# A delta-rule attention block and a hard-swish MLP on one core: eleven quarter products with w_in from the third block on, the sums of w_in moved to VectorE, and preparations moved between steps

## The chip, the cores and the metric

The kernel runs on one core of one Trainium2 chip. The metric is the device time of a launch in microseconds (us), as the median of several launches of the same program. TensorE (PE in the profile; PEld are its weight loads) multiplies matrices into PSUM. VectorE (DVE), ScalarE (ACT) and GpSimd (POOL) work beside it, and SyncE (SP) issues most of the DMAs. Each engine takes its instructions in the order in which the program lists them. An instruction that needs another engine's result waits for a semaphore, and all that is queued behind it on its own engine waits too.

## The reference

The first half is a delta rule over 768 tokens, for 4 batches and 8 heads of width 48. The second half is an MLP over the 3072 tokens that come out.

```python
k_n = k / (norm(k) + 1e-06)
for t in range(S):
    y[:, :, t] = einsum('bhd,bhde->bhe', q[:, :, t], state)
    v_old = einsum('bhde,bhd->bhe', state, kt)
    state = state + bt[:, :, :, None] * einsum('bhd,bhe->bhde', kt, vt - v_old)
x = y.transpose(0, 2, 1, 3).reshape(B * S, H * D)        # 3072 x 384
h = x @ w_in                                             # 384 x 2048
g = h * clip(h + 3.0, 0.0, 6.0) / 6.0
out = g @ w_out                                          # 2048 x 384
```

## The kernel before

**Chunks and steps.** The sequence is cut into 24 chunks of 32 tokens; a chunk of all four batches has 128 token rows. The loop at the end of the kernel has one *step* per chunk, from step 5 on; what comes before step 5 follows a written list of words (`ORDER`). In step t these parts are interleaved by hand in 15 *units* (u = 0 to 14):

- the chain of chunk t (`chain`): `ks` is the product with the state in unit 0; `R` is made on VectorE in units 1 and 2 and `y` in unit 3; `pz` follows in unit 4; the state's update `su` and the output product `py` in unit 8; `y` and the state's new value are made on VectorE in unit 9; `yt` transposes y in unit 10, and ScalarE copies it to `xT`, which is the MLP's input.
- the preparation of a later chunk (`prep`), in five stages: `kb` (the scaled keys, on GpSimd); four transposes of the keys (`pt`), their copy `KQ` on ScalarE and the `mask` (two GpSimd products into `mb`, which has one buffer); four transposes of the queries; the scores (`sc`, 64 small products); and `L` and `LB`, two VectorE products that read the scores and the mask, with `bkb` on GpSimd behind them. The stages are taken one by one: `now` is taken in units 1, 2, 4, 5 and 6, and the first stage of the next preparation (`later`) in unit 13. In a step that is listed in `APART`, scores and products come in units 6 and 7 in place of 4 and 5.
- a unit of the MLP (`mlp_units`) in each of the 15 units.
- *fill*: the norms of the keys of a later group of four chunks (four pairs of a GpSimd square `sq` and a VectorE sum `ss`, where `sq` has one buffer), or the inversion of the triangular matrices of the next group (`inverse`: a VectorE transpose of 1024 columns, 60 small VectorE products and subtractions, and a transpose back). Its pieces are spread over the units by a planned cost (`room`, `due`).

The scores of all preparations, `ks` and `su` share two PSUM slots (ring `pc`): `ks` and `su` each take both of them. All other products share four (ring `pm`). A slot is free when the instruction that reads it is done.

**The MLP.** A block is two chunks (256 tokens), so a block takes two steps. Its first half is `up`: for each of 16 column tiles of w_in there are 3 matmuls of 256 columns, and each of them is two instructions in the trace (96 for a block). ScalarE and VectorE then make the activation. `up_by_eleven` makes the same by a Strassen-like scheme: for each of 8 pairs of column tiles (j) there are seven products of 128 columns and two of 256 (18 instructions; 144 for a block). It takes 16 units, as `up` does. `begin(j)` issues four of the products, ScalarE copies them out, and GpSimd makes two sums (L1030, in `plus_minus`); `end(j)` issues the other five, then VectorE adds twice (L1093, L1097), and ScalarE and VectorE make the activation (L1110, L1113). It needs sums of w_in (`weight_sums`: S1, S2, S4, and W21 in place) and of the block's tokens (`token_sums`, on VectorE in unit 11). `UF` is the first block that is made this way.

The second half of a block is `down`; from block 2 on it is `down_by_seven`, a Strassen scheme with 7 of 8 products, in 14 units. It needs sums of w_out: 12 VectorE pieces (`quarters`, L1197) and four more in place (`last_quarter`, L1203). Block 1 still uses the plain `down` of 16 units; four of these come before step 5. In step 5 the units 0 to 11 are the rest of block 1's `down`, and block 2's `up` starts in unit 12. Each later block starts its `up` in unit 12 of an odd step as well.

**Places that the prediction names.** Before the change, steps 5 and 6 take two preparations each (chunks 9 and 10, then 11 and 12) and all later steps one. The inversion for chunks 9 to 12 (group 3) starts in unit 0 of step 7; in later groups it starts in unit 6 of the second step of a group (`ready`).

Of the kernel before, what the change touches and what calls it, by code (L numbers as in the profile page):

```python
# [44 lines left out]
def kernel(  # L45
# [969 lines left out]
                past.add(("up", blk))  # L1015
            yield

    UF = 4
    S1, S2, S4 = (sums_in[:, i] for i in range(3))

    def w_tiles(s, i):
# [7 lines left out]
    def plus_minus(out, a, b, op):  # L1029
        nc.gpsimd.tensor_tensor(out=out, in0=a, in1=b, op=op)  # L1030

    def weight_sums():
        for j in range(0, NPR, 2):
            r = slice(j, j + 2)
            plus_minus(S1[:, r], W21[:, r], W22[:, r], ALU.add)
            yield
            plus_minus(S2[:, r], S1[:, r], W11[:, r], ALU.subtract)
            yield
            plus_minus(S4[:, r], W12[:, r], S2[:, r], ALU.subtract)
            yield  # L1040
            plus_minus(W21[:, r], W11[:, r], W21[:, r], ALU.subtract)
            yield

    def x_tiles(blk):
        x = xTs[blk]
# [13 lines left out]
    def up_by_eleven(blk):  # L1059
        needs(("sums", blk))  # L1060
        B11, T3x, B21, B22, _, _ = x_tiles(blk)
        B3 = xTs[blk][:, 2].rearrange("p (i c) -> p i c", c=P)
        phs, ready = {}, {}

        def mm(ph, n, w, x, start=False, stop=False):
            nc.tensor.matmul(  # L1066
                ph[:, n], lhsT=w, rhs=x, start=start, stop=stop, skip_group_check=True
            )

        def begin(j):  # L1070
            key = ("ph", blk, "by", j)
            ring("pm", NPM, key)
            ph = phs[j] = psM.tile([128, 4, P], FP32, name="ph", tag=slot["pm"])
            mm(ph, 0, W11[:, j], B11, start=True)
            mm(ph, 1, S1[:, j], T1x)
            mm(ph, 2, W21[:, j], T3x)
            mm(ph, 3, S2[:, j], T2x)
            gs[blk, j] = g_all[:, 2 * j : 2 * j + 2]
            gt = gs[blk, j].rearrange("p i (t c) -> p (i t) c", c=P)
            nc.scalar.activation(out=gt, in_=ph[:], func=ACTF.Copy)  # L1080
            plus_minus(gt[:, 3:1:-1], gt[:, 0:2], gt[:, 3:1:-1], ALU.add)
            plus_minus(gt[:, 0], gt[:, 0], gt[:, 2], ALU.add)

        def end(j):
            ph = phs.pop(j)
            mm(ph, 0, W12[:, j], B21)
            mm(ph, 1, S4[:, j], B22)
            mm(ph, 2, W22[:, j], T4x)
            mm(ph, slice(0, 2), W13[:, j], B3)
            mm(ph, slice(2, 4), W23[:, j], B3, stop=True)  # L1090
            g = gs[blk, j].rearrange("p i c -> p (i c)")
            gt = gs[blk, j].rearrange("p i (t c) -> p (i t) c", c=P)
            nc.vector.tensor_tensor(  # L1093
                out=gt[:, 1:3], in0=ph[:, 1:3],
                in1=gt[:, 3].unsqueeze(1).to_broadcast([128, 2, P]), op=ALU.add,
            )
            nc.vector.tensor_tensor(out=gt[:, 3], in0=ph[:, 3], in1=gt[:, 0], op=ALU.add)  # L1097

            def first():
                nc.scalar.activation(out=gt[:, 0], in_=ph[:, 0], func=ACTF.Copy)  # L1100
                read(("ph", blk, "by", j))
                if j == 0 and blk < 9:
                    ready[j] = second
                else:
                    second()

            def second():
                ro = mlp.tile([128, CB, DM], FP32, name="o", bufs=1)
                r = ro[:].rearrange("p c m -> p (c m)")[:, 0 : 2 * TB]
                nc.scalar.activation(out=r, in_=g, func=ACTF.Relu, bias=half, scale=1.0 / 6.0)  # L1110

                def rest():
                    nc.vector.scalar_tensor_tensor(  # L1113
                        out=g, in0=r, scalar=1.0, in1=g, op0=ALU.min, op1=ALU.mult
                    )

# [12 lines left out]
        begin(1)  # L1129
        yield  # L1130
        for j in range(NPR):
            end(j)
            go(j - 1)
            if j + 2 < NPR:
                yield
                begin(j + 2)
                if j == 1:
                    go(0)
                go(j)
                yield  # L1140
# [156 lines left out]
    def mlp_units():  # L1297
# [21 lines left out]
        for blk in range(1, N // CB):  # L1319
            mode["of"] = "down"  # L1320
            mode["mean"] = 0.72 if blk + 1 < UF else 0.4
            sums = weight_sums() if blk == UF - 1 else iter(())
            for _ in downs(blk):
                next(sums, None)
                next(sums, None)
                yield
            if blk + 1 < N // CB:
                mode["of"] = "eleven" if blk + 1 >= UF else "up"
                for n, _ in enumerate((up_by_eleven if blk + 1 >= UF else up)(blk + 1)):
                    if blk + 1 == FIRST and n >= HF:  # L1330
                        drain(rest)
                        if n % 2:
                            last_quarter(n - HF - 1)
                    yield


# [9 lines left out]
    def drain(gen):  # L1346
        for _ in gen:
            pass
# [9 lines left out]
    def prep_of(t):  # L1358
        return made(("p", t), lambda: prep(t), t < N)
# [92 lines left out]
    with tc.manual_schedule():  # L1452
# [11 lines left out]
        loads = iter(())  # L1464
        left = due = 0
        USED = {"up": 0.42, "eleven": 1.0, "down": 0.7}
        APART = (12,)
        CHAIN = {0: 0.45, 1: 0.75, 2: 0.75, 3: 0.4, 4: 0.4, 6: 0.5, 9: 0.8, 10: 0.6, 14: 0.2}
        for t in range(LS, N):
            g, i = group(t)  # L1470
            ch = chain_of(t)
            behind = t - LS < LA - LE
            first_of = t + min(LA, LE + t - LS)
            now, more, later = (prep_of(first_of + n) for n in range(3))
            if not behind:
                more, later = (), more
            take(gens["v"], 4)
            if i == 0:
                left += 1
# [15 lines left out]
                13: lambda: take(later),  # L1495
            }
            if behind:
                for u in (7, 8, 10, 11, 12, 13):
                    plan[u] = lambda ch=plan.get(u): (ch and u < 13 and ch(), take(more))
                plan[14] = lambda: take(later)  # L1500
            ready = (2, 0) if behind or i == 2 and t - LS == LA - LE else (1, 6)
            for u in range(NU):
                if u in plan:
                    plan[u]()
                take(loads, 2)
                if (i, u) == (0, 2):
# [21 lines left out]
                due = min(due, 2.6)  # L1528
                take(fill, int(due))
                left, due = max(left - int(due), 0), due - int(due)  # L1530
            drain(ch)
        for _ in units:
            settle(2)
# [30 lines left out]
```

## Time and profile before

| what | us |
|---|---|
| median of 3 launches | 664.71 |
| lowest and highest of the 3 | 663.36, 664.77 |
| the profiled launch, its own time | 662.4 |
| the profiled launch, span from first to last instruction | 660.6 |
| TensorE busy | 633.3 |
| VectorE busy | 492.7 |
| ScalarE busy | 276.7 |
| GpSimd busy | 217.0 |

The profiled launch took 662.4 us, of which 660.6 us lie between its first and last instruction. In the lines below a time is in us from the start of that span. In the windows, the numbers of each stretch are the busy time of each engine, with the number of its instructions in brackets. In the timeline a line is: start, length, engine, line of the kernel, operation, tiles written and read, shape, count, and in square brackets the idle time of the engine just before and what ended it. The mean clock that TensorE was granted is 0.982.

The steps start, by the first `ks` matmul, at 152.6 (step 5), 179.9 (6), 207.2 (7), 232.8 (8), 258.6 (9), 283.8 (10), 308.6 (11), 333.7 (12) and 358.7 (13).

### The profile page before, as it was taken

Reading aid. Unit: us, or ns where it says so; the run is one execution under the profiler, and the core shown is the slowest. Engines: PE = TensorE matmul, PEld = TensorE weight load, DVE = VectorE, ACT = ScalarE, POOL = GpSimd, SP = SyncE. Lnnn points to the kernel's source line nnn. Section 1 sums busy time; section 2 is a strip of 40 time slices with the busy share of each in tenths; the row PEclk is TensorE's granted clock in tenths of the full one; section 3 lists DMA queues with packets and bytes.
Section 4 is the critical chain, followed back from the end, with each engine's and each line's share of the span. In section 5 each row is a group of like instructions: output and inputs, shape, how many; then the busy total and the mean of one; then the engine's idle time right before and its main releaser. Section 6 shows DMA issues by size and latency. Waiting matters only on the chain.

```text
span 660.6 us, 26484 instructions
## 1 busy us (share of the span) xinstructions
PE 633.3 (96%) x11592; PEld 567.8 (86%) x11592; DVE 492.7 (75%) x1158; ACT 276.7 (42%) x540; POOL 217.0 (33%) x336
## 2 busy tenths in 40 slices
PE   2768999999999999999999999999999999999997
PEld 2657987776789989999999999999999999999997
DVE  5899877798546698758988848989658998456354
ACT  5897689331243142154144244244244144153250
POOL 6531122003411363553254354164052241331430
PEclk9759999999999999999999999999999999999999
DMA  7888246212140030032030030030020020010000
GB/s 178 209 230 201 76 102 164 45 27 42 27 85 3 12 65 3 2 74 38 2 75 2 3 74 2 3 63 3 2 50 2 2 50 2 14 27 1 26 1 24
DMA packets 88691, 33.27 MB, mean 50 GB/s; under 512 B 80224, under 2 KB 83424, under 8 KB 88576
## 3 DMA queue, kind: packets, MB, share of 16 engines
q1 hardware_dynamic: 88224, 31.29, 21.1%
q8 instruction: 91, 1.49, 0.9%
q10 hardware_dynamic: 352, 0.30, 0.2%
q14 instruction: 24, 0.20, 0.1%
HBM read 26.84 MB, written 4.72 MB: 48 GB/s over the span
## 4 chain that ended last, share of the span: by engine, by line
PE 92%; ACT 3%; DVE 2%; DMA 2%; SPq 1%; issue 0%; ACTq 0%; DVEq 0%
PE po L1226 28%; PE ph L1066 24%; PE ph L994 12%; PE po L1162 6%; PE ks L806 4%; PE pt L524 3%; PE py L827 3%; PE pz L827 3%; PE sc L547 3%; PE su L938 3%; ACT spare L356 2%; DMA kf<-in_k_dram 1%; PE yt L873 1%; PE pi L684 1%; DVE pr L730 1%; DVE A L735 0%
## 5 line engine op out<-in xcount | busy, mean ns | idle before, releaser
L1066 PE MATMUL ph<-xT,w_in 128*128 128x128 f32 (+1 forms) x640 | 139.0, 321 | 0.0
L1226 PE MATMUL po<-w_out,g 128*128 128x192 f32 x640 | 110.6, 326 | 0.0
L1066 PEld LDWEIGHTS ph<-xT,w_in 128*128 128x128 f32 x640 | 104.0, 191 | 5.9
L1030 POOL TENSOR_TENSOR g<-g 128x256 f32<-128x256 f32 (+1 forms) x128 | 78.3, 613 | 92.8 <-ACT g L1080 87.8
L1226 PEld LDWEIGHTS po<-w_out,g 128*128 128x128 f32 x640 | 104.6, 190 | 0.5
L994 PE MATMUL ph<-xT,w_in 128*128 128x256 f32 (+1 forms) x480 | 93.3, 343 | 1.5 <-DVE g L1004 1.0
L1226 PE MATMUL po<-spare,g 128*128 128x192 f32 x480 | 86.7, 332 | 0.0
L994 PEld LDWEIGHTS ph<-xT,w_in 128*128 128x128 f32 x480 | 76.2, 190 | 11.5 <-DVE g L1004 1.3
L1226 PEld LDWEIGHTS po<-spare,g 128*128 128x128 f32 x480 | 77.2, 190 | 1.8
L1080 ACT ACTIVATE g<-ph 128x512 f32<-128x512 f32 x64 | 38.2, 597 | 92.8 <-PE ph L1066 92.8
L1236 POOL TENSOR_TENSOR o<-o,u 128x192 f32<-128x192 f32 x18 | 13.7, 762 | 165.9 <-ACT o L1233 87.9
L759 DVE TENSOR_TENSOR pr<-A 128x30 f32<-128x30 f32 (+9 forms) x150 | 58.8, 392 | 3.1
L1093 DVE TENSOR_TENSOR g<-ph,g 128x256 f32<-128x256 f32 x64 | 26.8, 419 | 44.4 <-PE ph L1066 39.5
L1212 DVE TENSOR_TENSOR g<-g 128x512 f32<-128x512 f32 x80 | 56.3, 724 | 4.6 <-PE po L1226 4.5
L764 DVE TENSOR_TENSOR A<-A,pr 128x30 f32<-128x30 f32 (+9 forms) x150 | 56.0, 373 | 3.5
L1001 ACT ACTIVATE g<-ph,halves 128x256 f32<-128x256 f32 (+1 forms) x80 | 33.7, 428 | 56.7 <-PE ph L994 56.7
L356 ACT ACTIVATE spare<-spare,places 128x768 uint16<-128x768 uint16 (+1 forms) x56 | 52.5, 942 | 2.3 <-DMA kf<-in_k_dram 1.2
L1113 DVE SCALAR_TENSOR_TENSOR g<-o,g 128x512 f32<-128x512 f32 x64 | 46.4, 725 | 6.8 <-ACT o L1110 6.8
L1110 ACT ACTIVATE o<-g,halves 128x512 f32<-128x512 f32 x64 | 46.2, 723 | 10.5 <-DVE g L1113 7.8
L1066 PE MATMUL ph<-beta_tok,sums_in 128*128 128x128 f32 x256 | 49.5, 275 | 0.0
L1233 ACT ACTIVATE o<-po 128x192 f32<-128x192 f32 x40 | 13.2, 330 | 82.9 <-PE po L1226 79.3
L510 POOL TENSOR_TENSOR kb<-kf,inv 128x384 f32<-128x384 f32 x24 | 21.7, 905 | 74.0 <-issue 43.1
(141 smaller groups left out, 1022.0 us busy)
## 6 DMA issues: line engine op xcount, KB each, us to landing
kf<-in_k_dram SPq DMA_DIRECT2D x96, 48.0 KB, 2.5
qb<-in_q_dram SPq DMA_DIRECT2D x96, 48.0 KB, 2.7
vf<-in_v_dram SPq DMA_DIRECT2D x96, 48.0 KB, 2.0
out_dram<-o SPq DMA_DIRECT2D x90, 48.0 KB, 1.6
spare<-in_moe_w_in_dram SPq DMA_DIRECT2D x4, 768.0 KB, 5.3
w_out<-in_moe_w_in_dram SPq DMA_DIRECT2D x4, 768.0 KB, 5.6
w_out<-in_moe_w_out_dram SPq DMA_DIRECT2D x4, 768.0 KB, 7.4
spare<-in_moe_w_out_dram SPq DMA_DIRECT2D x4, 768.0 KB, 5.0
```

The source lines that it names most:

```text
L356: nc.scalar.activation(out=z, in_=z if n else d.bitcast(I16)[:, :, :, 3], func=func, bias=places[:, n : n + 1], scale=scale,)
L759: nc.vector.tensor_tensor(out=pv, in0=A[:, j + 1 :, j].unsqueeze(2).to_broadcast([n, w, j]), in1=A[:, j, 0:j].unsqueeze(1).to_broadcast([n ...
L764: nc.vector.tensor_tensor(out=A[:, j + 1 :, 0:j], in0=A[:, j + 1 :, 0:j], in1=pv, op=ALU.subtract)
L827: nc.tensor.matmul(ps[rows(place(b)), D * h : D * h + D], lhsT=m(h)[rows(b)], rhs=z[rows(b), D * at(h) : D * at(h) + D], start=True, stop= ...
L994: nc.tensor.matmul(ph[:, cols], lhsT=w_in[:, s, f * 128 : (f + 1) * 128], rhs=xT[:, s, cols], start=(s == 0), stop=(s == NKT - 1),)
L1030: nc.gpsimd.tensor_tensor(out=out, in0=a, in1=b, op=op)
L1066: nc.tensor.matmul(ph[:, n], lhsT=w, rhs=x, start=start, stop=stop, skip_group_check=True)
L1110: nc.scalar.activation(out=r, in_=g, func=ACTF.Relu, bias=half, scale=1.0 / 6.0)
L1113: nc.vector.scalar_tensor_tensor(out=g, in0=r, scalar=1.0, in1=g, op0=ALU.min, op1=ALU.mult)
L1162: nc.tensor.matmul(pos[c][:], lhsT=gs[blk, f // 2][:, f % 2, c * P : (c + 1) * P], rhs=w_out[:, f, :], start=(f == 0), stop=(f == NFC - 1),)
L1212: nc.vector.tensor_tensor(out=A(f, *out, 4), in0=A(f, *a, 4), in1=A(f, *b, 4), op=op)
L1226: nc.tensor.matmul(ps[n][:], lhsT=A(f - f % 2, *a)[:, f % 2], rhs=b[:, f], start=(f == 0), stop=(f == HF - 1),)
```

## The change

- `UF` is 2 in place of 4: blocks 2 and 3 also use the eleven products.
- The 16 pieces of w_in's sums are made by VectorE, no longer by GpSimd, and two blocks earlier: they begin in the ninth unit of block 1's `down` (unit 4 of step 5), one per unit, two per unit from its thirteenth unit on, and the last four come beside the first four units of block 2's `up`.
- The last pieces of w_out's sums come two units earlier.
- Step 5 takes three preparations (chunks 9, 10, 11) and the first stage of the fourth behind its last unit; step 6 takes only the rest of that fourth one (chunk 12). In step 5 the preparation of chunk 10 has its stages in units 3, 5, 6, 7 and 8 (ahead of `su`), that of chunk 11 in units 9 to 13.
- The inversion of group 3 starts in unit 6 of step 6, as later groups do.
- Step 8 is added to `APART`.

```diff
-    UF = 4
+    UF = 2
...
     def weight_sums():
         for j in range(0, NPR, 2):
             r = slice(j, j + 2)
-            plus_minus(S1[:, r], W21[:, r], W22[:, r], ALU.add)
-            yield
...
+            for out, x, y, op in (
+                (S1, W21, W22, ALU.add), (S2, S1, W11, ALU.subtract),
+                (S4, W12, S2, ALU.subtract), (W21, W11, W21, ALU.subtract),
+            ):
+                nc.vector.tensor_tensor(out=out[:, r], in0=x[:, r], in1=y[:, r], op=op)
+                if out is W21:
+                    past.update((("ws", j), ("ws", j + 1)))
+                yield
...
         def begin(j):
             key = ("ph", blk, "by", j)
+            needs(("ws", j))
...
-            for _ in downs(blk):
-                next(sums, None)
-                next(sums, None)
+            for n, _ in enumerate(downs(blk)):
+                if n >= 8:
+                    next(sums, None)
+                if n >= 12:
+                    next(sums, None)
                 yield
...
                 for n, _ in enumerate((up_by_eleven if blk + 1 >= UF else up)(blk + 1)):
-                    if blk + 1 == FIRST and n >= HF:
+                    next(sums, None)
+                    if blk + 1 == FIRST and n >= HF - 1:
                         drain(rest)
-                        if n % 2:
-                            last_quarter(n - HF - 1)
+                        if n % 2 and n < 2 * HF - 2:
+                            last_quarter(n - HF + 1)
...
-        APART = (12,)
+        APART = (8, 12)
...
-            behind = t - LS < LA - LE
-            first_of = t + min(LA, LE + t - LS)
-            now, more, later = (prep_of(first_of + n) for n in range(3))
+            behind = t == LS
+            now, more, third, later = (prep_of(t + LA - n) for n in (2, 1, 0, -1))
             if not behind:
-                more, later = (), more
+                now = third
...
             if behind:
-                for u in (7, 8, 10, 11, 12, 13):
-                    plan[u] = lambda ch=plan.get(u): (ch and u < 13 and ch(), take(more))
-                plan[14] = lambda: take(later)
-            ready = (2, 0) if behind or i == 2 and t - LS == LA - LE else (1, 6)
+                plan[13] = None
+                for u, gen in zip((3, 5, 6, 7, 8, 9, 10, 11, 12, 13), (more,) * 5 + (third,) * 5):
+                    plan[u] = lambda old=plan.get(u), gen=gen, first=u == 8: (
+                        first and take(gen), old and old(), first or take(gen)
+                    )
+            ready = (1, 6)
...
+            if behind:
+                take(later)
             drain(ch)
```

More of the change, by code (lines that the diff above doesn't have):

```diff
@@ L1034, in weight_sums @@
             r = slice(j, j + 2)
-            plus_minus(S1[:, r], W21[:, r], W22[:, r], ALU.add)
-            yield
[L1037 to L1042, printed above, removed]
+            for out, x, y, op in (
[6 more added lines that the diff above has]
+                yield
     def x_tiles(blk):
@@ L1497 @@
             if behind:
-                for u in (7, 8, 10, 11, 12, 13):
-                    plan[u] = lambda ch=plan.get(u): (ch and u < 13 and ch(), take(more))
-                plan[14] = lambda: take(later)
-            ready = (2, 0) if behind or i == 2 and t - LS == LA - LE else (1, 6)
+                plan[13] = None
[4 more added lines that the diff above has]
+            ready = (1, 6)
             for u in range(NU):
-                if u in plan:
+                if plan.get(u):
                     plan[u]()
```

## The prediction

> **What bounds the kernel now.** I read the page first, then the waits of TensorE, the windows of single steps, the chain of waits, and last the timelines of the stretches that the change touches.
>
> ```profile
> PE 633.3 (96%) x11592; PEld 567.8 (86%) x11592; DVE 492.7 (75%) x1158; ACT 276.7 (42%) x540; POOL 217.0 (33%) x336
> ...
> PE 92%; ACT 3%; DVE 2%; DMA 2%; SPq 1%; issue 0%; ACTq 0%; DVEq 0%
> ```
>
> TensorE is busy for 96% of the span and carries 92% of the chain that ended last. Asked for the waits from 90 us on, the view lists none for PE matmuls, and the starts of neighbouring matmuls show no hole there. So from step 4 on the end is set by how much TensorE has to issue; a preparation, an inversion or a sum that comes earlier gains nothing by itself, and it costs nothing as long as no matmul waits for it. The windows of steps 5 to 10 show the same (columns: PE, PEld, DVE, ACT, POOL).
>
> ```profile
> 152.60:179.90 27.30, 27.30 (x473) 18.78 (x472) 17.98 (x44) 5.92 (x12) 13.47 (x17) 1.00 0.11 25
> 179.90:207.20 27.30, 27.30 (x498) 23.69 (x497) 14.45 (x31) 10.20 (x21) 5.23 (x7) 1.00 0.33 59
> 207.20:232.80 25.60, 25.60 (x446) 24.00 (x445) 17.48 (x43) 5.25 (x12) 6.82 (x10) 1.00 0.05 14
> 232.80:258.60 25.80, 25.79 (x426) 22.14 (x425) 25.11 (x62) 9.20 (x19) 13.72 (x18) 1.00 0.19 36
> 258.60:283.80 25.20, 25.20 (x454) 23.81 (x453) 17.90 (x39) 5.81 (x13) 11.91 (x14) 1.00 0.04 11
> 283.80:308.60 24.80, 24.80 (x466) 22.86 (x465) 17.98 (x41) 12.74 (x26) 13.80 (x22) 1.00 0.35 66
> ```
>
> PE fills each stretch. VectorE has 9 to 13 us to spare in steps 5 and 6 and almost none in step 8.
>
> **What the eleven products save.** Steps 7 and 8 hold block 3 with the plain `up` and last 25.6 + 25.8 = 51.4 us. Steps 9 and 10 hold the same chains and one preparation each, with the eleven products: 25.2 + 24.8 = 50.0 us; steps 11 and 12 take 50.1. That is 1.35 us for a block. The chain of waits gives it without the surroundings:
>
> ```profile
> 184.69 2.59 PE ph L994 x12
> ...
> 619.52 19.47 PE ph L1066 x144
> ```
>
> Twelve instructions (two column tiles) of the plain form take 2.59 us, eight pairs 20.72; the eleven form takes 19.47 for the eight: 1.25 us less. Two blocks give 2.5 to 2.8 us; I take 2.7.
>
> Behind this stands a spacing that halves with the columns: 2.59 / 12 = 216 ns for 256, and (2.43 - 4 x 0.216) / 14 = 112 ns for 128. A rule of the Trainium skill speaks against this change: TensorE: Matmul & The Clock Gate, Back-to-back issue gap, gives a sustained 81 ns at 128 columns and 131 ns at 512, so halving the columns saves less than half. An estimate by that page (98 ns at 256, on the line between) would make a pair 14 x 81 + 4 x 98 against 12 x 98 ns, 0.35 us dearer, and 16 pairs 5.6 us, near 670. The trace disagrees with it for these f32 products.
>
> **The sums of w_in on VectorE.** There are 16 instructions of 128x256. The nearest rows are L1093 (128x256, 419 ns) and L1197 (128x384, 537 to 658 ns), so 0.42 to 0.55 each, 6.7 to 8.8 us in all; GpSimd loses its 13.4 us (L1030 with w_in). Twelve lie in step 5, one or two per unit, where VectorE would stand idle before the sums of squares anyway (below). TensorE needs the first four only seven units later. I cost them at nothing on TensorE's path in step 5; without that cover each second one would delay what is queued behind it by 0.4 us. The token sums of block 2 (L1056, 1.6 us) come in unit 11 of step 5; from `yt` to block 2's first product TensorE now has 0.44 + 1.30 + 0.44 + 1.30 + 0.79 = 4.3 us of other work, where block 4 had 2.6 and did not wait: nothing.
>
> **Three preparations in step 5.** The number of preparations in steps 5 and 6 stays four, 1.67 us of TensorE each (0.44 + 0.44 + 0.79), so TensorE's work does not change. No load moves: the written list issues 48 query loads, which are chunks 0 to 11, and the last landed at 149.7. What changes is who waits in step 5. Scores of chunk 10 now stand in unit 7, and `su` in unit 8 needs both `pc` slots, so it waits for `LB` of chunk 10. Before, `su` came ahead of these scores. In VectorE's queue the norms stand ahead of that `LB`:
>
> ```profile
> 163.45 1.07 POOL L409 TENSOR_TENSOR sq<-kf 128x384 f32<-128x384 f32 x1 [5.75 <-DMA out_dram<-o]
> ...
> 167.90 0.82 POOL L409 TENSOR_TENSOR sq<-kf 128x384 f32<-128x384 f32 x1
> ...
> 175.52 1.19 POOL L486 TENSOR_TENSOR mb<-beta_tok,mask 128x256 f32<-128x256 f32 x2 [5.23 <-DVE nt L426]
> ```
>
> ```profile
> 162.03 0.41 DVE L558 TENSOR_TENSOR LB<-sc,mb 128x256 f32<-128x256 f32 x1
> ...
> 168.75 0.55 DVE L413 TENSOR_REDUCE ss<-sq 128x8 f32<-128x384 f32 x1 [1.29 <-POOL sq L409]
> ```
>
> Nothing moves before 162.4, when `LB` of chunk 9 ends. The mask of chunk 10 (one buffer) can start 0.15 later and lasts 1.19: 163.8. Only then comes the first square, which before had been ready at 157.7: 0.82, so the first `ss` starts at 164.6. Square and sum alternate through one buffer: 0.55 + 1.07 to 1.20 + 0.12, so 1.74 to 1.87 apart, and the third `ss` starts at 168.1 to 168.4. `L` and `LB` of chunk 10 follow: 0.47 + 0.34 + 0.41 + 0.1 = 1.3, so 169.4 to 169.7. TensorE is ready for `su` at 161.5 + 1.39 + 1.74 + 1.74 + 2.18 = 168.56. It waits 0.9 to 1.1 us; I take 1.0. With squares of 0.82 throughout it is 0.4, with a mask of 1.56 and squares of 1.27 it is 1.9.
>
> **Step 6 as a copy of step 10.** Step 6 now holds what step 10 holds (eleven products, inversion from unit 6, one preparation), so its rows price it. Two things differ. First, `kb` of chunk 12 is behind step 5's last unit, so behind `bkb` of chunk 11 and the second pair of GpSimd sums; in step 9 it stood ahead of that pair:
>
> ```profile
> 283.36 0.83 POOL L510 TENSOR_TENSOR kb<-kf,inv 128x384 f32<-128x384 f32 x1
> 284.15 1.26 POOL L1030 TENSOR_TENSOR g<-g 128x256 f32<-128x256 f32 x2
> ```
>
> Counted from block 4's first product (280.38), the first pair of sums (282.14 to 283.40) ends at 3.0; then 0.82 + 1.26 + 0.83 with short gaps make `kb` ready at 6.1. TensorE reached those key transposes at 285.92, so at 5.5: a wait of 0.6 (0.3 to 0.9, since `kb` took 0.82 to 1.14).
>
> Second, two pieces of w_out's sums (L1203, 0.47 to 0.95 of the queue each) stand in units 6 and 8 ahead of `y`:
>
> ```profile
> 300.82 0.55 DVE L863 TENSOR_TENSOR y<-y,py 128x384 f32<-128x384 f32 x1
> ```
>
> ```profile
> 301.66 0.49 PE L873 MATMUL yt<-ident,y 128*128 128x128 f32 x3
> ```
>
> In step 10 y is done at 301.37, 0.2 before it would be late, and VectorE had no gap since 296.8. With 0.94 more in front, `yt` waits about 0.7 (0.4 to 1.3).
>
> VectorE's load in step 6 is 14.45, plus 4.9 for the eleven form (8 x (0.42 + 0.29 + 0.73) against 16 x 0.41), plus 1.7 for the last four sums, less 0.8 for a preparation, plus about 5.5 of inversion: some 25 of 26 us. In step 8 it falls by that inversion's share, and step 8 resembles step 12 (same `APART` order, 25.0 us), whose longest listed wait is `su` for `LB`, 0.3 us: nothing beyond the 50.1 that I used.
>
> **The sum.** Saved 2.7; waits 1.0 + 0.6 + 0.7 = 2.3 (1.1 to 4.1 with all bounds). Net -0.4: the profiled launch would go from 662.4 to 662.0, and the median, which lies 2.3 above that launch, from 664.71 to 664.3. A difference of 0.2% (1.3 us) is about what a measurement of this kernel can tell from no change.
>
> **The rivals.** *The waits do not form* (faster). VectorE runs ahead where I let it wait, for instance because squares take 0.82 (one of three did in step 5), and y's slack is larger. With one or no wait left the time is 662.0 to 663.3. For it: steps 9 to 14 hold no PE wait at a VectorE share of 70 to 90%. Against it: the order of the queues leaves the first two waits little room. It needs waits below 1.4 in sum. Chance 0.33.
>
> *VectorE becomes the bound of step 6* (slower). Beside GpSimd its rows stretch: L1197 was 0.54 to 0.85, L1113 0.68 to 1.00. At 25 of 26 us, a tenth more is 2.5 us that no gap takes up, and all of it stands ahead of y; `yt` then waits 0.7 + 2.0, and with 1.0 and 0.6 before it the waits are 4.3: 666.3. It decides once the waits exceed 2.7 + 1.3 = 4.0. The Trainium skill (GPSIMD Engine Reference, table of its properties) says that GpSimd's SBUF access contends with VectorE instructions that have two SBUF inputs, which all of these have; the spread of those rows agrees. Chance 0.19.
>
> *Small products are paced by their weight loads* (slower). A weight load takes 0.19 us in every row (104.0 us for 640 in L1066). If these followed one another, a pair would cost 18 x 0.19 = 3.42 against 2.59 us, and 16 pairs 13 us more: about 678. But 144 instructions in 19.47 us are 135 ns each, so the loads overlap. Chance 0.01. The skill's page above, whose spacing is set by load and product together, points the same way.
>
> *The change does not do what it says*: `UF` is read for every block, so this has no chance that I can count.
>
> **How the numbers follow.** My case, net within 1.3 of zero, gets the rest, 0.47. Its own range is 663.4 to 666.0. The range 662.1 to 666.3 takes in most of both neighbours and leaves out about 2 in 10.
>
> **What would show it.** In the profile after, steps 7 and 8 last 50.0 to 50.2 us; L1066 has 1440 matmul records and the plain form loses 192. PE has a hole of about 1 us before `su` in step 5, ended by `LB`; one of 0.6 before `pt` early in step 6, ended by `kb`; one of 0.7 before `yt` there, ended by y. Steps 5 and 6 together last 54.6 - 1.4 + 2.3 = 55.5 us; 53.2 would be the first rival, over 57 the second. Holes in steps 7 and 8, or a lower granted clock, would make me wrong for a reason that I do not have.

## The result and the profile after

The changed kernel takes 666.45 us (median of 14 launches, 664.64 to 668.98); the kernel before, launched in turn with it on the same chip, takes 663.74 us (14 launches, 662.27 to 665.44). That is 1.0 us below the 664.71 of three launches from which the prediction counted. The ratio is 1.0036, 95% interval 1.0023 to 1.0049: slower by 1.5 to 3.3 us. The profiled launch took 666.5 us, with a span of 664.8 us.

The page first, the same two lines as before (busy time of each engine, then the chain that ended last by engine):

```profile
PE 630.6 (95%) x11688; PEld 567.9 (85%) x11688; DVE 510.9 (77%) x1198; ACT 286.1 (43%) x556; POOL 223.6 (34%) x352
...
PE 87%; DVE 5%; DMA 2%; issue 2%; SPq 1%; POOL 1%; ACT 1%; POOLq 0%; DVEq 0%
```

From step 5 to the end, by the windows of these two stretches, TensorE is busy for 502.7 us in place of 504.6, and yet the stretch lasts 509.3 us in place of 508.0. VectorE, which had 2% of the chain, has 5%. The windows say where (steps 5, 6, 7 and 8; columns PE, PEld, DVE, ACT, POOL):

```profile
155.44:185.50 30.06, 29.00 (x554) 20.24 (x553) 26.06 (x62) 7.48 (x14) 14.38 (x18) 1.00 0.07 17
185.50:212.40 26.90, 25.18 (x468) 22.78 (x467) 21.50 (x47) 12.73 (x26) 15.36 (x23) 1.00 0.34 62
212.40:237.50 25.10, 25.10 (x458) 23.87 (x457) 22.87 (x55) 6.21 (x13) 4.82 (x9) 1.00 0.04 12
237.50:262.50 25.00, 25.00 (x470) 22.78 (x469) 21.32 (x52) 12.62 (x26) 14.62 (x22) 1.00 0.21 41
```

Steps 7 and 8 last 50.1 us (51.4 before) and PE fills them. In steps 5 and 6, 57.0 us (54.6 before), the first two columns differ: 1.1 and 1.7 us in which PE does nothing. The waits of TensorE from 150 us to the end name them (total, times, longest, in us); the view of before had none:

```profile
PE yt L873 <- DVE y L863: 1.3, 1, 1.3
PE su L938 <- DVE LB L558: 1.1, 1, 1.1
PE po L1227 <- issue: 0.4, 1, 0.4
PE pt L524 <- POOL kb L510: 0.4, 1, 0.4
```

Three of the four are the waits that the prediction named, at their places (172.95, 188.10 and 205.38 us) and with their releasers. The fourth, ended by nothing that the profile shows, stands at 472.8 us. A wait in this view is less than what it costs, because the modelled end of the matmul before lies inside it. Counted from start to start, above the usual spacing of these matmuls, the four are 1.16 (`su`), 0.57 (`pt`), 1.48 (`yt`) and 0.59 us (`po`). The expectations and the text below use this count and call it a hole.

### The profile page after: what moved, and what is told of

Same layout as the page of the kernel before. It is cut to its first block, busy times and chain, and to the rows that moved or that the text cites. A ratio compares the mean times of both kernels' runs of the same rounds, so it can differ in the third digit from the quotient of the medians.

```text
span 664.8 us, 26792 instructions
## 1 busy us (share of the span) xinstructions
PE 630.6 (95%) x11688; PEld 567.9 (85%) x11688; DVE 510.9 (77%) x1198; ACT 286.1 (43%) x556; POOL 223.6 (34%) x352
## 4 chain that ended last, share of the span: by engine, by line
PE 87%; DVE 5%; DMA 2%; issue 2%; SPq 1%; POOL 1%; ACT 1%; POOLq 0%; DVEq 0%
PE ph L1066 29%; PE po L1227 28%; PE ph L994 6%; PE po L1163 6%; PE ks L806 3%; PE su L938 3%; PE pz L827 3%; PE py L827 3%; PE pt L524 3%; PE sc L547 2%; PE yt L873 1%; SPq L168 1%; DMA w_out<-in_moe_w_in_dram 1%; DMA spare<-in_moe_w_in_dram 1%; PE pi L684 1%
## 5 line engine op out<-in xcount | busy, mean ns | idle before, releaser
L1066 PE MATMUL ph<-xT,w_in 128*128 128x128 f32 (+1 forms) x800 | 174.4, 321 | 0.0
L1030 POOL TENSOR_TENSOR g<-g 128x256 f32<-128x256 f32 (+1 forms) x160 | 98.4, 616 | 124.3 <-ACT g L1081 118.0
L1066 PEld LDWEIGHTS ph<-xT,w_in 128*128 128x128 f32 x800 | 129.7, 191 | 7.5
L1081 ACT ACTIVATE g<-ph 128x512 f32<-128x512 f32 x80 | 47.8, 597 | 114.9 <-PE ph L1066 114.9
L1094 DVE TENSOR_TENSOR g<-ph,g 128x256 f32<-128x256 f32 x80 | 33.6, 419 | 52.3 <-PE ph L1066 48.8
L1114 DVE SCALAR_TENSOR_TENSOR g<-o,g 128x512 f32<-128x512 f32 x80 | 58.8, 736 | 8.5 <-ACT o L1111 8.5
L1111 ACT ACTIVATE o<-g,halves 128x512 f32<-128x512 f32 x80 | 57.8, 723 | 12.9 <-DVE g L1114 9.7
L1066 PE MATMUL ph<-beta_tok,sums_in 128*128 128x128 f32 x320 | 61.9, 275 | 0.0
L764 DVE TENSOR_TENSOR A<-A,pr 128x30 f32<-128x30 f32 (+9 forms) x150 | 53.7, 358 | 3.1
L994 PE MATMUL ph<-xT,w_in 128*128 128x128 f32 (+1 forms) x288 | 48.9, 317 | 1.8 <-DVE g L1004 1.1
L1066 PEld LDWEIGHTS ph<-beta_tok,sums_in 128*128 128x128 f32 x320 | 48.6, 192 | 0.0
L994 PEld LDWEIGHTS ph<-xT,w_in 128*128 128x128 f32 x288 | 40.8, 191 | 7.0 <-DVE g L1004 1.5
```

Source lines behind the costliest of these rows:

```text
L764: nc.vector.tensor_tensor(out=A[:, j + 1 :, 0:j], in0=A[:, j + 1 :, 0:j], in1=pv, op=ALU.subtract)
L994: nc.tensor.matmul(ph[:, cols], lhsT=w_in[:, s, f * 128 : (f + 1) * 128], rhs=xT[:, s, cols], start=(s == 0), stop=(s == NKT - 1),)
L1066: nc.tensor.matmul(ph[:, n], lhsT=w, rhs=x, start=start, stop=stop, skip_group_check=True)
L1114: nc.vector.scalar_tensor_tensor(out=g, in0=r, scalar=1.0, in1=g, op0=ALU.min, op1=ALU.mult)
```

## The theories

A: the three waits on TensorE's path in steps 5 and 6, 3.2 us against some 2.6 saved, make the difference. B: the changed program is slower outside these steps, by the loading of TensorE's instructions (B1) or by a later start of step 5 (S). C: VectorE is too full in steps 5 to 8, and a wait that is taken away comes back elsewhere.

The table has all runs. "5 to 8" is the time from the first `ks` of step 5 to that of step 9 in the profiled launch, "9 to end" the rest of the span, both in us; the ratio is against the kernel before on the same chip.

| kernel | median us | ratio and interval | start of step 5 | 5 to 8 | 9 to end |
|---|---|---|---|---|---|
| before (first profile) | 663.74 | | 152.59 | 106.05 | 401.95 |
| before2 (the same) | 664.19 | 1.0005, 0.9990 to 1.0020 | 155.38 | 106.05 | 402.23 |
| after (first profile) | 666.45 | 1.0036, 1.0023 to 1.0049 | 155.44 | 107.03 | 402.29 |
| after2 (the same) | 666.7 | 1.0029, 1.0015 to 1.0044 | 153.72 | 107.06 | 402.59 |
| sq_act | 666.33 | 1.0020, 1.0002 to 1.0038 | 155.86 | 106.33 | 403.83 |
| all3 | 664.64 | 1.0005, 0.9988 to 1.0022 | 154.42 | 105.75 | 403.89 |
| eleven_only | 669.28 | 1.0074, 1.0048 to 1.0100 | 154.32 | 106.84 | 407.92 |
| preps_only | 666.60 | 1.0033, 1.0019 to 1.0048 | 153.69 | 108.23 | 402.32 |
| shift32 | 669.59 | 1.0085, 1.0059 to 1.0111 | 159.23 | 107.15 | 401.66 |
| best1 | 666.50 | 1.0036, 1.0015 to 1.0057 | 158.62 | 104.53 | 402.02 |
| late32 | 665.84 | 1.0024, 1.0008 to 1.0039 | 155.28 | 107.05 | 402.30 |
| pool_lq | 663.07 | 0.9980, 0.9961 to 0.9999 | 156.91 | 104.24 | 402.32 |
| best2 | 662.17 | 0.9962, 0.9948 to 0.9977 | 156.47 | 104.18 | 401.75 |

The start of step 5 scatters by some 3 us between launches of the same program. The time of steps 5 to 8 comes back within 0.05 us where the program is the same (one of eight profiles differs, below), so the experiments are read there.

## Experiments

### Both kernels once more (before2, after2)

> The kernel before, against itself: ratio 1.000 within 0.001. Theory A: its start of step 5 also moves by 1 to 3 us between profiles. Theory B: step 5 starts at 152 to 153 us again.

> The changed kernel once more, to part its steps from its start. Theory A (three waits on TensorE's path in steps 5 and 6, 3.3 us, against 2.7 us saved; the rest is how a launch happens to start): steps 5 to 8 last 107 us again, the waits before su, pt and yt are again 1.3, 0.6 and 1.5 us, and the start of step 5 differs freely between profiles; some 1 us slower than before in steps 5 to 8. Theory B (the changed program is also slower outside of these steps): step 5 starts about 3 us later than 152.6 again, and steps 9 to 23 last longer than the 402.0 us of before.

Measured: 106.05 against 107.06 us in steps 5 to 8, and 402.23 against 402.59 us behind them. The holes are 1.16, 0.57, 1.47, and 0.88 us ahead of `po`. So steps 5 to 8 cost the change 1.0 us, twice over.

### One wait taken away (sq_act)

```diff
-            if g < 4:
+            if g < 5:
                 nc.scalar.activation(out=sq[:], in_=kf[:, i0 + i], func=ACTF.Square)
```

> The changed kernel with the squares of the norms of step 5 (group 4) on ScalarE in place of GpSimd, so that they no longer stand behind the mask of chunk 10. Theory A: the wait of su in step 5 falls from 1.3 us to under 0.3, and the kernel gains 1.0 to 1.3 us on the changed one. Rival C (VectorE has too much to do in step 5, whoever makes the squares): L and LB of chunk 10 are as late, or the wait returns before py, yt or the first eleven product; gain under 0.4.

The squares of group 4 are made by ScalarE, no longer by GpSimd. The hole ahead of `su` is gone, those ahead of `pt` and `yt` stay at 0.57 and 1.46, and steps 5 to 8 are 0.7 us shorter than in the changed kernel. The time did not follow: behind the start of step 9 stands a hole of 1.32 us ahead of two `sc` products at 272.4 us, again ended by nothing that the profile shows.

This run also prices VectorE's sums of w_in. In the changed kernel, VectorE and then GpSimd from the first to the third sum of squares, and `LB` behind them:

```profile
168.74 1.05 DVE L1039 TENSOR_TENSOR sums_in<-w_in,sums_in 128x256 f32<-128x256 f32 x1
169.71 0.54 DVE L413 TENSOR_REDUCE ss<-sq 128x8 f32<-128x384 f32 x1
...
170.64 1.04 DVE L1039 TENSOR_TENSOR w_in<-w_in 128x256 f32<-128x256 f32 x1
...
172.39 0.41 DVE L558 TENSOR_TENSOR LB<-sc,mb 128x256 f32<-128x256 f32 x1
```

```profile
168.43 1.07 POOL L409 TENSOR_TENSOR sq<-kf 128x384 f32<-128x384 f32 x1 [0.67 <-DVE ss L413]
170.32 1.07 POOL L409 TENSOR_TENSOR sq<-kf 128x384 f32<-128x384 f32 x1 [0.82 <-DVE ss L413]
```

In sq_act the same two sums have no GpSimd instruction beside them:

```profile
169.32 0.41 DVE L1039 TENSOR_TENSOR sums_in<-w_in,sums_in 128x256 f32<-128x256 f32 x1
...
170.58 0.41 DVE L1039 TENSOR_TENSOR w_in<-w_in 128x256 f32<-128x256 f32 x1
```

0.41 us alone, 1.05 beside a square: the prediction's bounds of 0.42 to 0.55 held for the engine alone. The difference is a wait and not a slower pace: both long rows end 0.29 us after the square that was running when they began (169.50 and 171.39). In the traces of all runs, 80 of these sums began while a GpSimd instruction had more than 0.1 us left, and 79 of them end 0.28 to 0.29 us after it. The row of the same size by which the prediction set its lower bound, L1093 (L1094 in the changed kernel), has one input in PSUM: it takes 0.38 to 0.43 us whether GpSimd runs beside it or not, so it could not show this price.

### All three waits taken away (all3)

```diff
 # sq_act, and:
+                plan[13] = lambda: (take(third), take(later))
...
-            if behind:
-                take(later)
...
-                        if n % 2 and n < 2 * HF - 2:
-                            last_quarter(n - HF + 1)
+                        if n >= 12:
+                            last_quarter(2 * (n - 12))
```

> The changed kernel with one edit against each wait: squares of group 4 on ScalarE, kb of chunk 12 ahead of step 5's second pair of GpSimd sums (unit 13), and the last four pieces of w_out's sums in the last four units of block 2's up. Theory A: the waits of su and pt are under 0.3 us, that of yt 0.5; about 2.7 us faster than the changed kernel, 1.5 us (0.2%) faster than before. Rival C: the waits appear elsewhere in steps 5 to 8, and these steps last 106 us or more.

`kb` of chunk 12 now stands ahead of the second pair of GpSimd's sums, and w_out's last four pieces behind y. All three holes are gone. Step 6 falls from 26.9 to 24.8 us, but step 7 grows from 25.1 to 26.4: the last of these pieces now stands in step 7 (the first line below), VectorE reaches R late, and TensorE waits for that. With the four pieces off VectorE (pool_lq and best2, below) 0.2 to 0.3 us of this wait are left.

```profile
211.65 0.55 DVE L1204 TENSOR_TENSOR w_out<-w_out 128x384 f32<-128x384 f32 x1
```

```profile
217.05 0.88 PE L827 MATMUL pz<-R,X 32*32 32x48 f32 x64 [1.17 <-DVE R L909]
```

A is right on the three waits, and C is partly right: one came back, with 1.32 us counted from start to start. The `sc` hole of 1.34 us behind the start of step 9 is there again. The time equals that of the kernel before; 1.5 us less was expected.

### The two halves of the change alone (eleven_only, preps_only)

eleven_only has the preparations, the inversion and `APART` as before the change; preps_only is the kernel before with only these three changed.

```diff
 # eleven_only, against the changed kernel
-        APART = (8, 12)
+        APART = (12,)
...
-            behind = t == LS
+            behind = t - LS < LA - LE
...
-            ready = (1, 6)
+            ready = (2, 0) if behind or i == 2 and t - LS == LA - LE else (1, 6)
```

```diff
 # preps_only, against the changed kernel
-    UF = 2
+    UF = 4
...
-                nc.vector.tensor_tensor(out=out[:, r], in0=x[:, r], in1=y[:, r], op=op)
+            plus_minus(S1[:, r], W21[:, r], W22[:, r], ALU.add)
```

> The changed kernel with the preparations, the inversion and the order of steps 7 and 8 as before the change: only the eleven products from block two on and VectorE's sums of w_in remain. Theory A (three waits on TensorE's path, made by the moved preparations and by what VectorE and GpSimd then have queued): no wait of TensorE for LB ahead of su in step 5; steps 5 to 8 last 104.7 to 105.5 us (106.05 before, 107.03 after). Theory C (VectorE has no room for the eleven form in these steps, wherever the preparations stand): one or two waits of 1 us or more for VectorE come up in step 7 or 8, where the inversion now lies beside eleven products, and steps 5 to 8 last 106 us or more.

The wait of `su` for `LB` is gone, as A says, but `yt` in step 8 waits 1.7 us for y, and the worst comes in step 9. This is the wait there, and the clock around it (the last three numbers of a window are PE's granted clock, the DMA share and GB/s):

```profile
PE pz L827 <- DVE X L473: 2.5, 1, 2.5
```

```profile
269.00:271.00 2.00, 0.00 (x0) 0.00 (x0) 2.00 (x2) 0.00 (x0) 1.38 (x2) 0.90 0.00 0
271.00:274.00 3.00, 2.94 (x129) 2.69 (x130) 2.48 (x6) 0.49 (x1) 0.00 (x0) 0.50 0.00 0
```

The inversion is not done when its result is due, TensorE stands still for 2.5 us, and then runs at half clock until about 277.4 us: products of 192 columns start 320 ns apart there and 163 ns afterwards. Step 9 takes 30.4 us in place of 25.1, so the lower clock costs as much as the hole itself. The Trainium skill (TensorE: Matmul & The Clock Gate, section on the HAM clock gate) puts the half clock behind an idle window of about 3.4 us; here 2.5 us without a matmul were enough. So C holds for the eleven products alone: without the earlier inversion they are 4.75 us slower than the kernel before. The moved preparations and the earlier inversion, which this run takes back together, are a condition of the eleven products here and not an addition.

> The kernel before with only the change's preparations, inversion and order of steps (blocks two and three plain, sums of w_in on GpSimd where they were). Theory A: su in step 5 waits for LB, 0.6 to 1.1 us, without any sum of w_in on VectorE; the wait of pt for kb in step 6 is gone, since GpSimd has no sums of products ahead of it; yt waits less than 0.5. Steps 5 to 8 last 106.6 to 107.4 us, time 664.7 to 665.6 beside 664.2 before. If it is VectorE's sums of w_in beside GpSimd that make the wait ahead of su, there is none here, and steps 5 to 8 last 106.0 to 106.3.

`su` waits for `LB`, and `pt` and `yt` do not wait, as A says:

```profile
170.71 0.84 PE L938 MATMUL su<-R,bkb 32*64 32x48 f32 x60 [0.56 <-DVE LB L558]
```

Counted from start to start the hole is 0.67 us, against 1.16 with VectorE's sums of w_in in the queue. The sums that I had costed at nothing are therefore 0.5 of the 1.16. Steps 5 to 8 came out 0.8 us above the upper end that I gave, and the time 1.0 us above: 0.92 of the 108.23 us is a hole ahead of `py` at 252 us that is of the next kind.

### The hole that nothing ends (shift32, late32)

TensorE's instructions are loaded by a queue of their own; on the page after it is this line (packets, MB, share):

```profile
q8 instruction: 92, 1.51, 0.9%
```

Its packets are of 16 KB. The holes without a releaser stand, with few exceptions, at record 193 of each 256, when the trace's matmuls, weight loads and the 192 other records of TensorE's queue (189 semaphore instructions and 3 drains) are numbered together: 1473, 2753, 4801, 10689, 18113. The changed kernel has 23568 such records and 92 packets. So 16 KB are 256 records; each 256 are called a piece below, and the place between two pieces a border. Ahead of the `po` hole in step 17 of the changed kernel, 246 of the 256 records of `pz` and `sc` lie in one piece; TensorE uses them up in 1.6 us, and the whole piece in 2.3:

```profile
469.73 0.88 PE L827 MATMUL pz<-R,X 32*32 32x48 f32 x64
470.54 0.86 PE L547 MATMUL sc<-KQ 64*32 64x64 f32 x64
471.33 1.08 PE L1227 MATMUL po<-spare,g 128*128 128x192 f32 x5
472.84 2.06 PE L1227 MATMUL po<-spare,g 128*128 128x192 f32 x11 [0.43 <-issue]
```

Two kernels move the borders by 32 records: shift32 by 16 transposes more early in the kernel, late32 by 8 score products more at 123 us.

```diff
 # shift32
-            for p in range(NP):
+            for p in [*range(NP)] * (3 if t == 1 else 1):
                 nc.tensor.transpose(
 # late32
-        for p in range(NP):
+        for p in [*range(NP)] + [0] * (t == 8):
             for b in range(B):
```

> The changed kernel with the eight transposes of chunk 1 made three times over (16 more products, far ahead of step 5), so that every later instruction of TensorE stands 32 records further on. Theory B1 (the hole of 0.6 to 0.9 us ahead of po at 472 us is a border between two pieces of TensorE's instructions, which come in pieces of 256 records, and it shows because all small products of step 17 fill just one piece): the hole goes, the three waits in steps 5 and 6 stay (1.16, 0.57, 1.47), steps 5 to 8 last 107.0 us, and from step 9 to the end 401.7 to 402.0 us in place of 402.3 to 402.6. If the hole belongs to those instructions themselves, it stays at its place with 0.6 to 0.9 us.

The same stretch in shift32:

```profile
474.51 0.86 PE L547 MATMUL sc<-KQ 64*32 64x64 f32 x64
475.30 2.87 PE L1227 MATMUL po<-spare,g 128*128 128x192 f32 x16
```

No hole over 0.2 us there or anywhere behind the start of step 5 but the three waits, and 401.66 us from step 9 on: B1 stands. But the early borders moved as well: holes of 0.68, 0.96, 0.70 and 1.74 us at 73.8, 86.0, 98.2 and 103.0 us delay step 5 to 159.2, and the kernel is 3 us slower than the changed one.

> The changed kernel with eight of the small score products of chunk 8 (at about 123 us) made twice, 32 more records of TensorE behind the borders at 98 and 102 us, where the run with 16 transposes more lost time. Theory B1 (a hole comes where 256 records of small products fill one piece of instructions): no hole ahead of po at 472 us and none at the other borders after step 9; the start of step 5 lies at 153 to 156 us, steps 5 to 8 last 107.0 us with the same three waits, step 9 to the end 401.6 to 401.9 us; the time is 0.5 to 1 us below that of the changed kernel, some 665.5 us, and what is left against the kernel before is the 1.0 us of steps 5 to 8. Otherwise the hole stays, or another comes, and the time is 666.4 us.

Shifted behind those borders, the `po` hole is gone and step 5 starts at its usual time, but a smaller hole (0.43 us) stands ahead of `py` at 303.1 us, at another border, so that step 9 to the end takes 402.30 us and not the 401.6 to 401.9 expected. shift32 has its borders at the same records and had none there, so a border can show in one launch and not in another. The median, 665.84 us, is 0.6 to 0.9 below the changed kernel's; the intervals of these comparisons overlap.

The trace also records each packet of this queue, and these records tell the two cases apart. In the 17 traces TensorE passes none of the 1543 borders sooner than 1.24 us after the packet of the piece behind it has landed, and the holes at borders named here all end 1.2 to 1.6 us after that: the `po` hole of the changed kernel ends at 472.84 us, and its packet ran from 470.48 to 471.44. After 62 us most packets start 0.4 to 2 us behind the border before theirs, too late for a piece that is used up in about 2.4 us; a quarter start ahead of that border. The packet of the `py` hole in late32 started 0.65 us behind the border before; in shift32 the same packet started 0.05 us behind it, and no hole came. So each of these holes is a late packet. Why a packet starts early in one launch and late in another was not found.

### A version without the waits (best1, pool_lq, best2)

```diff
 # pool_lq: squares and kb as in all3, and the last four pieces of w_out's sums by GpSimd
-        nc.vector.tensor_tensor(
-            out=B12[:, f : f + 2], in0=B22[:, f : f + 2], in1=B12[:, f : f + 2], op=ALU.subtract
-        )
+        plus_minus(B12[:, f : f + 2], B22[:, f : f + 2], B12[:, f : f + 2], ALU.subtract)
...
-                        if n % 2 and n < 2 * HF - 2:
-                            last_quarter(n - HF + 1)
+                        if n % 2 and n > HF:
+                            last_quarter(n - HF - 1)
 # best1: pool_lq with the edit of shift32; best2: pool_lq with that of late32
```

> The changed kernel with the squares of group 4 on ScalarE, kb of chunk 12 ahead of the second pair of GpSimd's sums, the last four pieces of w_out's sums on GpSimd in units 6, 8, 10 and 12 of step 6, and the 32 records of shift. Theory A: none of the three waits, and the wait of 1.32 us ahead of pz in step 7, which came up where the same four pieces stood later in VectorE's queue, does not form, as VectorE loses 2 us; steps 5 to 8 last 104.4 to 105.0 us, the holes at instruction borders after step 9 are gone, and the time is 662 to 663.2 beside 664.2 before. Theory C (no room in VectorE): a wait of 1 us or more for VectorE stands in step 6, 7 or 8, steps 5 to 8 last 105.5 us or more, and the time is 664 or above.

> The changed kernel with the squares of group 4 on ScalarE, kb of chunk 12 ahead of the second pair of GpSimd's sums, and the last four pieces of w_out's sums on GpSimd; no shift of the records. Theory A: steps 5 to 8 last 104.5 us with one wait of 0.4 us left (pz for R in step 7); theory B1: the holes at 472 us (0.6 to 0.9) and perhaps at 271 us (1.3) stay, step 9 to the end lasts 402.3 to 403.9 us. Time 663.0 to 664.2.

> The kernel of pool_lq with the 32 records at 123 us as well. Theories A and B1 together: steps 5 to 8 last 104.5 us, step 9 to the end 401.7 to 402.1 us, no hole over 0.5 us behind step 5; started at 153 to 156 us as the kernel before, the time is 662.0 to 663.2, that is 1.5 us (0.2%) less than before. If the start comes as late as in the two runs with the shift far ahead of step 5 (158 to 159 us), it is 665 to 666.

Steps 5 to 8 take 104.2 to 104.5 us in all three. best1 lost 4 us ahead of step 5, as shift32 did, so its time missed what was expected. pool_lq keeps the `po` hole (0.59 us) and is at the edge of a difference; best2 has no hole at a border behind the start of step 5 and is faster than both kernels, by 1.5 to 3.5 us against the kernel before. Its profiled launch, which came to step 5 late (156.47 us), is the slowest of its twelve (664.13 us), so the gain is that of the medians and of steps 5 to 8. Its waits of TensorE behind step 5, and its steps 5 and 6:

```profile
PE pz L827 <- DVE R L909: 0.3, 1, 0.3
```

```profile
156.47:185.40 28.93, 28.93 (x553) 20.21 (x552) 24.91 (x62) 9.36 (x18) 10.20 (x14) 1.00 0.09 21
185.40:210.20 24.80, 24.80 (x469) 22.86 (x468) 19.53 (x41) 12.35 (x25) 17.16 (x25) 1.00 0.37 66
```

Against the changed kernel, steps 5 and 6 fall from 57.0 to 53.7 us, nearly all of it the 3.2 us of the three holes. C is wrong for the whole: there is room, in VectorE once GpSimd takes 2 us of it, and in GpSimd.

### Further profiles of both kernels (look_a1, look_a2, look_a3, look_b1)

> The changed kernel again, one look. Steps 5 to 8 107.0 us with the three waits. Theory B1 (what is left of the difference lies in holes at borders of TensorE's instructions, which differ from launch to launch): a hole of 0.6 to 0.9 us ahead of po at 472 us in each look, and in some of the three a second one of 1.3 us ahead of sc in step 9 (at 271 us); then the mean of step 9 to the end is 402.8 us or more. Theory S (the start is later): no further hole, and step 5 starts a microsecond or more later than in the looks of the kernel before (152.6 and 155.4).

> The changed kernel, a second further look: the same expected of it as of the first one (B1: po hole of 0.6 to 0.9 us, perhaps one of 1.3 us ahead of sc; S: only a later start).

> The changed kernel, a third further look: the same expected of it as of the first one (B1: po hole of 0.6 to 0.9 us, perhaps one of 1.3 us ahead of sc; S: only a later start).

> The kernel before again, one look. Theory B1: no hole at a border after step 5, step 9 to the end 401.9 to 402.3 us; steps 5 to 8 106.05 us. Theory S: step 5 starts at 152.5 to 154.5 us.

In the three profiles of the changed kernel step 5 starts at 154.16, 154.48 and 153.52 us, steps 5 to 8 last 107.06, 107.36 and 107.04, the rest 402.60, 402.60 and 402.30. The `po` hole is there each time (0.87, 0.87, 0.59 us); the `sc` hole never came. In that of the kernel before: 153.25, 106.06 and 402.53 us, with one hole of 0.45 us at a border at 419.9 us, which B1 had not expected (before2 has 0.25 us at the same border).

Over five profiles of the changed kernel and three of the kernel before, the means differ by 0.5 us in the start of step 5 (154.26 against 153.74), by 1.06 in steps 5 to 8 (107.11 against 106.05) and by 0.24 behind them (402.48 against 402.24), 1.8 us in all. The starts scatter by more than 0.5 us, so this part is not shown to be the change's; the holes at borders between 62 us and step 5 come to 0.0 to 1.4 us in either kernel, on average 0.8 before and 0.6 after, and do not make it. The medians differ by 2.5 to 2.7 us with intervals from 1.0 and 1.5 us on; what lies between 1.8 and that stays open.

## Why the prediction was right or wrong

**The saving** was forecast well: 1.3 us in steps 7 and 8 (50.1 us, forecast 50.0 to 50.2). In steps 5 and 6 the starts of the `ph` matmuls in best2, which has no hole there, sum to 20.17 us for 144 against 21.42 for 96 in the kernel before: 1.25. Of it 0.2 goes to the plain `down` of block 1, whose matmuls alternate with other forms ten times in place of seven. L1066 has 800 + 320 + 160 + 160 = 1440 matmul records, and L994 lost 192. The spacing rule of the Trainium skill that spoke against the change did not decide: steps 7 and 8 became shorter.

**The wait of `su`** (1.0 forecast, 1.16 measured) came out near by luck, by two errors that cancelled. The chain of squares and sums alone gives 0.67 (preps_only), less than I had, and the sums of w_in that I costed at nothing on TensorE's path give the other 0.5: this is the first step that failed. One of them stands behind each of the first two sums of squares, where VectorE is idle for 0.72 us without them (preps_only). That covers 0.41 us, but not the 1.05 that a sum lasts when it has to wait for the square.

**The wait of `pt`** (0.6 forecast, 0.57 measured) was right, and its place in GpSimd's queue as well: with `kb` ahead of the second pair it is gone.

**The wait of `yt`** is the second step that failed, and the larger one: the term of 0.7 (0.4 to 1.3) measured 1.48. That step 6 is a copy of step 10 was right: without the two pieces (all3) `yt` starts 17.82 us after the first `ks` of its step, as in step 10 of the kernel before. In that step 10 the last two inversion pieces ahead of y are done when GpSimd starts its pair of sums:

```profile
300.43 0.22 DVE L759 TENSOR_TENSOR pr<-A 128x58 f32<-128x58 f32 x1
300.68 0.22 DVE L764 TENSOR_TENSOR A<-A,pr 128x58 f32<-128x58 f32 x1
```

```profile
301.00 1.26 POOL L1030 TENSOR_TENSOR g<-g 128x256 f32<-128x256 f32 x2 [2.96 <-ACT g L1080]
```

In the changed kernel the pieces of w_out's sums push them into it. VectorE ahead of y, and GpSimd beside it:

```profile
203.03 0.55 DVE L1204 TENSOR_TENSOR w_out<-w_out 128x384 f32<-128x384 f32 x1
203.49 0.74 DVE L759 TENSOR_TENSOR pr<-A 128x58 f32<-128x58 f32 x1
204.27 0.50 DVE L764 TENSOR_TENSOR A<-A,pr 128x58 f32<-128x58 f32 x1
204.69 0.54 DVE L863 TENSOR_TENSOR y<-y,py 128x384 f32<-128x384 f32 x1
```

```profile
203.24 1.46 POOL L1030 TENSOR_TENSOR g<-g 128x256 f32<-128x256 f32 x2 [2.96 <-ACT g L1081]
```

The two inversion pieces took 0.74 and 0.50 us; in all3, without GpSimd beside them, the same two take 0.22 each. That is 0.80 us more, and 1.48 less 0.80 is the 0.7 of the sum. So the second rival's mechanism (rows of VectorE that stretch beside GpSimd, ahead of y) worked, at less than half of the 2.0 us that I gave it: the waits reach 3.2, not the 4.0 from which it was to decide, and steps 5 and 6 came to 56.95 us, at the edge of the 57 that was to show it. VectorE was also not as full as that rival had it: 21.5 of 26.9 us in step 6, in place of some 25 of 26. The contention that the prediction cites from the Trainium skill (GPSIMD Engine Reference) is borne out by these rows and by those of the sums. It is not a stretch in proportion: in the traces of all runs, the 17 rows of 128x58 that began while a GpSimd instruction had more than 0.1 us left end 0.08 us after it. I kept this price in a rival. The rows of before showed that it belonged in the sum: the two pieces end 0.1 us ahead of GpSimd's pair, and 0.94 us was to come in front of them.

**The sum.** Forecast for steps 5 to 8: 2.7 saved, 2.3 waited, 0.4 us faster. Measured: 2.55 saved, 3.2 waited, 0.2 for the alternation, and 0.2 that is left over (most of it in the products of `su` in step 5, which take 1.86 us in best2 and 1.64 before): 1.05 us slower. This is 1.45 of the 3.1 us between the forecast difference of -0.4 and the measured 2.7; 0.24 more, the border holes behind the start of step 9, had no step in the prediction at all. The cause of the other 1.4 us stays open: 0.5 is the start of step 5, which scatters by more than that, and the rest shows in no profile. The first rival (waits that do not form) is refuted. The rival of products paced by weight loads is too: steps 7 and 8 keep the saving in full.

## What to carry to other kernels

When work is moved onto an engine that stands close to the path, price each instruction as it runs beside its neighbour on the other engine, not by its fastest row, and put that price into the sum. For a VectorE sum or product of two SBUF tiles it was here what was left of the GpSimd instruction that ran when it began; a row with an input in PSUM did not show it. A change that is right in TensorE's work can be lost in the order of two other queues: here three pieces of work given to another engine or another place, and one shifted border, turned a loss of 2.5 us into a gain of 2.5 us. Where TensorE stops with nothing that ends the wait, number its records, and look when the packet of the next piece landed: a border between pieces of its instructions may have moved into a run of small products.

## What the runs showed of the hardware that I had not expected

- TensorE's instructions come in pieces of 16 KB, 256 records of the trace. At a border behind a piece that is used up in about 2.4 us or less TensorE can stop, behind the start of step 5 for 0.4 to 1.3 us, and goes on 1.2 to 1.6 us after the next piece has landed. Of kernels with the same order of instructions some show a given border and some do not, as the packet starts late or early (in sq_act and all3 the piece behind the `sc` hole was loaded 4 us later than in the changed kernel); what makes it start early was not found.
- A hole of 2.5 us in TensorE was followed by 6 us at half clock (eleven_only), so that it cost twice its length. Holes up to 1.9 us (ahead of `yt` in step 8 of the same run) left the clock at 1.00.
- A VectorE sum of 128x256 with both inputs in SBUF takes 0.41 us alone and up to 1.05 when it begins beside a GpSimd square of 128x384: it ends 0.28 us after the square. The square itself takes 1.07 us in place of 0.82 when it begins beside a VectorE piece of w_out's sums; this stands in preps_only too, without sums of w_in.
